# Eight of block 1's first products of layer 1 set among block 0's, their h kept where layer 2's weights will lie

## The chip, the cores and the metric

The kernel runs on one core of a Trainium2 chip. The metric is the device time of one launch in microseconds (us). Engines work from queues of their own, in the order in which the program lists each engine's instructions, and wait for each other by semaphores: PE does matrix products into PSUM, ACT and DVE do the work on single elements, SP issues the transfers (DMA). The profile's names are used throughout: PEld is PE's load of the fixed operand, which runs beside a product before it.

## The reference

`x` has the shape (2, 4096, 192), in single precision; the weights of the two layers come in double precision.

```python
w = softmax(weight, axis=-1)                   # (8 heads, 7 taps)
x_pad = pad(x, 6 zeros ahead of each sequence)
conv[b, s, h, g] = sum_k w[h, k] * x_pad[b, s + k, h, g]   # causal, 24 channels of a head
x = conv.reshape(8192, 192)

g = x @ w_gate                                 # layer 1: 192 -> 1536
x = (g * sigmoid(g) * (x @ w_val)) @ w_out     # 1536 -> 192

h = x @ w_in                                   # layer 2: 192 -> 2048
out = where(h > 0, h, exp(min(h, 0)) - 1) @ w_out2         # 2048 -> 192
```

## The kernel before

**Tiling.** Tokens lie along the free axis, channels on the partitions. The 8192 tokens are 16 blocks of `TB` = 512. Layer 1 of a block has 12 units of 128 of the 1536 middle channels, layer 2 has 16 units, taken two by two. Every operand of a product is split in a high and a low part of the number format `fp32r` (hi, lo), and a product is hi·hi + lo·hi + hi·lo.

**Couples.** A product of PE uses 64 of the 128 rows of the array. Two of them, one for the lower 64 rows and one for the upper, run side by side and write to two banks; this pair of matmuls is called a couple. A layer-1 unit has 9 couples of *first products* (`nine`, L362: gate columns into bank `pg`, value columns into `pv`), and 5 couples of *second products* (`ten`, L405) which add the unit's part to the block's four sums `c`. Between them stand silu (ACT L672), the gate (DVE L676), h hi (ACT L646) and h lo (DVE L650). A pair of layer-2 units has 9 couples into two banks `ph`, then per unit tanh (L706) and exp (L710) on ACT, `less` (L714) and `bound` (L718) on DVE, h hi and lo, and 2 x 5 couples of second products.

**Room.** PSUM has four banks `a` for first products (two units or pairs in flight) and four for `c`. Parts of h have a ring of 5 tiles each, `t` one of 4. A block's operand, hi and lo, has three homes.

**Weights.** They come as 34 pieces: 12 of W1 (first products of layer 1, one per unit), 6 of O1 (second products, one per two units), 8 of W2 and 8 of O2 for layer 2. SP brings a piece's words (L262) into a ring of 4; ACT and DVE make the parts from them: scale (ACT L266), three (ACT L289), join (DVE L293), sign (DVE L274), then hi (ACT L298) and lo (DVE L301). The pieces come in the order O1 0, W1 0, W1 1, W1 2, W1 3, O1 1, W1 4, ... and those of layer 2 last, W2 and O2 in turn.

**Order.** Layer and block follow in stages (1,0), (1,1), (1,2), (2,0), (2,1), (1,3), (2,2), (1,4), (2,3), ... up to (1,15), (2,14), (2,15). PE's order is fixed as the code writes it; for ACT, DVE and SP a planner places each instruction when by its costs its operands are there, the one with the longest tail first. Second products go through the list `due`: after each unit's first products all but the newest entry of `due` are written; at a stage's last unit before a layer-2 stage (`hold`) none are, so that they fill the first pairs of that stage. The convolution of block 1, taps (L576) and the operand's parts (L449, L453, L473, L477), stands in block 0's stage, that of block 2 in block 1's.

In the text, A b.j is a unit's first products in block b of layer 1, o b.j its second products, and E b.k a pair's first products of layer 2. PE's order at the start is A0.0, A0.1, A0.2, o0.0, A0.3, o0.1, ... A0.11, A1.0 and so on to A2.11, and then E0.0, o2.9, o2.10, E0.1, o2.11, E0.2.

Of the kernel before, what the change touches and what calls it, by code (L numbers as in the profile page):

```python
# [18 lines left out]
TB = 512  # L19
SLOTS = (0, 2, 1)  # L20
LEAD = 3
AIDED = 1
PATIENCE = 0.05
EPS = 2.0**-16
SPARED = range(0, 34)


def raw(ap):
    return ap.bitcast(F32)
# [103 lines left out]
def tile_conv_swiglu_elu(ctx: ExitStack, tc: tile.TileContext, x, weight, words, out, FF1, FF2):  # L133
# [10 lines left out]
    NU = {1: FF1 // P, 2: FF2 // P}  # L144
    assert D == P + HALF and TB % 2 == 0
    C = 2 * D
# [21 lines left out]
    plan = Plan()  # L168

    def act(emit, needs=(), new=(), uses=(), pitch=0.52, ready=0.68):  # L170
        return plan.add("act", pitch, ready, emit, needs, new, uses)

    def dve(emit, needs=(), new=(), uses=(), pitch=0.61, ready=0.74):
        return plan.add("dve", pitch, ready, emit, needs, new, uses)
# [72 lines left out]
    ready = {}  # L247

    def piece(k, moves, halves, serves):
# [34 lines left out]
        def three():  # L284
# [3 lines left out]
            w = box["st"].bitcast(U32)[:, :, 0]  # L288
            nc.scalar.activation(out=w, in_=w, func=AF.Copy, scale=2.0**-29 * (1 - EPS), bias=7.5 * EPS - 0.5)  # L289

# [122 lines left out]
    W1, W2 = Into("in1", NU[1]), Into("in2", NU[2] // 2)  # L413
    O = {1: OutOf("out1", NU[1]), 2: OutOf("out2", NU[2])}
# [145 lines left out]
    def conv(b, g):  # L560

        n = blocks[b][2]
        m, c0 = ((n, 0), (n // 2, HALO + TB))[g]
        src, src_b, came = xs[b]
        acc_b = plan.buffer("cv", 2)
        box = {}

        def tap(k):
            s = src["t"][:, c0 + k : c0 + k + m]
            w = taps[:, g, k : k + 1]  # L570
            if k == HALO:
                box["acc"] = cv_p.tile([P, TB], F32, tag="cv", name=f"cv{b}_{g}")
                nc.scalar.mul(box["acc"][:, :m], s, w)
                return
            acc = box["acc"][:, :m]
            nc.vector.scalar_tensor_tensor(out=acc, in0=s, scalar=w, in1=acc, op0=ALU.mult, op1=ALU.add)  # L576

        less = 0.0 if g == 0 else 0.27
        t = act(lambda: tap(HALO), [made, *came[g]], new=[acc_b], uses=[src_b], pitch=0.62 - less, ready=0.78 - less)
        for k in range(HALO):  # L580
            t = dve(lambda k=k: tap(k), [t], uses=[src_b, acc_b], pitch=0.67 - less, ready=0.8 - less)
        if g == 0:
            if b not in X:
                X[b] = Operand(f"x{b}", home["x", b])
            X[b].write(0, lambda: box["acc"][:, :n], [t], [acc_b], n)
        else:
            X[b].spread(lambda: box["acc"], t, acc_b, n)
# [29 lines left out]
    live = {}  # L617
    parts = {}
    split_of = {}
    sums = {}  # L620
    turns = {"last": None}

    def func(t):

        if turns["last"]:
            t.behind.append(turns["last"])
        turns["last"] = t
        return t

    def load_table(f):  # L630
        func(act(lambda: table(f), pitch=1.3, ready=1.3))

    def split(u):

        layer, b, j = u
        n = blocks[b][2]
        t_b, done = live[u][1:]
        bufs = [plan.buffer(f"h{q}", 5) for q in ("hi", "lo")]
        parts[u] = [None, None]

        def make(q):
            parts[u][q] = h_p.tile([P, TB], F32R, tag=f"h{'hi lo'.split()[q]}", name=f"h{q}_{layer}_{b}_{j}")

        def hi():
            make(0)
            nc.scalar.copy(parts[u][0][:, :n], live[u][0]["t"][:, :n])  # L646

        def lo():
            make(1)
            nc.vector.tensor_tensor(  # L650
                out=parts[u][1][:, :n], in0=live[u][0]["t"][:, :n], in1=raw(parts[u][0][:, :n]), op=ALU.subtract
            )

        h = act(hi, [done], new=[bufs[0]], uses=[t_b])
        l = dve(lo, [done, h], new=[bufs[1]], uses=[bufs[0], t_b])
        split_of[u] = bufs, (h, l)

    def swiglu(b, j):

        n = blocks[b][2]  # L660
        ps_b = [plan.buffer("a", 4) for _ in range(2)]
        t_b = plan.buffer("t", 4)
        box = {}

        def banks():
            if "p" not in box:
                box["p"] = [ps_a.tile([P, TB], F32, tag="a", name=f"p{q}{b}_{j}") for q in "gv"]
            return box["p"]

        def silu():  # L670
            box["t"] = t_p.tile([P, TB], F32, tag="t", name=f"t1_{b}_{j}")
            nc.scalar.activation(out=box["t"][:, :n], in_=box["p"][0][:, :n], func=AF.Silu)  # L672

        def gate():
            t = box["t"][:, :n]
            nc.vector.tensor_tensor(out=t, in0=t, in1=box["p"][1][:, :n], op=ALU.mult)  # L676

        last = W1.nine(ps_b, banks, j, X[b], n)[-1]
        s = func(act(silu, [last], new=[t_b], uses=ps_b[:1], pitch=0.49, ready=0.64))
        m = dve(gate, [last, s], uses=[ps_b[1], t_b])  # L680
        live[1, b, j] = box, t_b, m
        split((1, b, j))
# [46 lines left out]
    def products_out(u):  # L729
        layer, b, j = u  # L730
        n = blocks[b][2]
        if j == 0:
            second = [plan.buffer("c", 4) for _ in range(2)]
            acc_b[layer, b] = [plan.buffer("c", 4) for _ in range(2)] + second
        tasks = O[layer].ten((layer, b), acc_b[layer, b], j, u, n)
        if j == NU[layer] - 1:
            (middle if layer == 1 else finish)(b, *tasks)
# [88 lines left out]
    products(1)  # L826
    load_table(AF.Silu)

    due = []
    for i, (layer, b) in enumerate(stages):  # L830
        if i + 1 < len(stages) and stages[i + 1][0] == 1:
            if i:
                load_x(stages[i + 1][1])
            conv(stages[i + 1][1], 0)
            if i >= AIDED:
                conv(stages[i + 1][1], 1)
        if i and stages[i - 1][0] != layer:
            load_table(AF.Silu if layer == 1 else AF.Exp)
        for j in range(0, NU[layer], layer):
            swiglu(b, j) if layer == 1 else elus(b, j // 2)  # L840

            hold = layer == 1 and j == NU[1] - 1 and i + 1 < len(stages) and stages[i + 1][0] == 2
            while len(due) > 1 and not hold:
                for u in due.pop(0):
                    products_out(u)
            due.append([(layer, b, j + a) for a in range(layer)])
    for us in due:
        for u in us:
            products_out(u)

    plan.run({"pe": 1.0, "act": 0.8, "dve": 1.0, "pool": 2.3, "sp": 0.8}, PATIENCE)


# [43 lines left out]
```

## Time and profile before

| | us |
|---|---|
| median of 3 runs | 1224.89 (1224.43 to 1225.32) |
| the profiled execution | 1225.62 |
| its span | 1223.9 |
| PE busy | 1207.8 (99%) |
| DVE busy | 981.4 (80%) |
| ACT busy | 833.7 (68%) |
| chain that ended last: PE's part | 92% |

```profile
PE   7999999999999999999999999999999999999998
PEclk9999999999999999999999999999999999999999
DVE  7999899788595986959779596895968869495697
```

Each digit is the busy share of a fortieth of the span (30.6 us) in tenths. PE stands still only in the first slice, which holds the start of the program and the first weights; from there on it is busy at full clock. A time without PE's work can be saved only where PE waits.

### The profile page before, as it was taken

What the parts mean: (1) busy time and instruction counts of PE and PEld (TensorE: products, weight loads), DVE (VectorE), ACT (ScalarE), POOL (GpSimd) and SP (SyncE); (2) the same over time, 40 slices, a digit from 0 to 9 for tenths busy, and PEclk for the clock granted to TensorE, in tenths of its full rate; (3) what the DMA queues carried; (4) which work ended last, traced back from release to release, by engine and by line L of the source; (5) the groups of instructions that cost most, each with busy time, mean ns of one, the idle gap of its engine ahead of it and who ended that gap; (6) DMA issues with size and microseconds to landing.
All of it is one profiled execution on the core that took longest, in us unless ns stands there. A gap on an engine that the chain in (4) does not pass through costs nothing.

```text
span 1223.9 us, 25338 instructions
## 1 busy us (share of the span) xinstructions
PE 1207.8 (99%) x10272; PEld 968.8 (79%) x10272; DVE 981.4 (80%) x1631; ACT 833.7 (68%) x1556; POOL 2.1 (0%) x15
## 2 busy tenths in 40 slices
PE   7999999999999999999999999999999999999998
PEld 5778888888888888788887888878878788888876
DVE  7999899788595986959779596895968869495697
ACT  6979687486583856748576484765848667485676
POOL 0000000000000000000000000000000000000000
PEclk9999999999999999999999999999999999999999
DMA  6644020202020020201102011020200102000000
GB/s 174 192 128 125 15 44 14 66 18 53 1 44 27 18 53 8 49 15 25 47 10 48 14 36 36 18 53 1 44 14 18 40 1 47 12 18 14 18 11 18
DMA packets 34917, 48.65 MB, mean 40 GB/s; under 512 B 5872, under 2 KB 19696, under 8 KB 34800
## 3 DMA queue, kind: packets, MB, share of 16 engines
q1 hardware_dynamic: 34784, 47.04, 15.1%
q8 instruction: 80, 1.31, 0.5%
q14 instruction: 37, 0.30, 0.1%
q10 hardware_dynamic: 16, 0.00, 0.0%
HBM read 19.75 MB, written 6.29 MB: 21 GB/s over the span
## 4 chain that ended last, share of the span: by engine, by line
PE 92%; DVE 3%; ACT 2%; SPq 1%; DMA 1%; issue 1%; ACTq 0%; DVEq 0%
PE c L405 40%; PE pv L362 30%; PE ph L362 21%; DMA words<-in_words_dram 1%; SPq L262 1%; DVE t L714 1%; DVE t L718 1%; PE pg L362 0%; DVE w L293 0%; DVE h L650 0%; ACT w L266 0%; DVE t L676 0%; ACT words L289 0%; SPq L518 0%; DVE in1lo L301 0%
## 5 line engine op out<-in xcount | busy, mean ns | idle before, releaser
L405 PE MATMUL c<-h,out 64*128 64x512 f32 x4480 | 639.4, 392 | 0.5 <-DVE o L755 0.4
L405 PEld LDWEIGHTS c<-h,out 64*128 64x128 f32 x4480 | 472.9, 185 | 104.6 <-DVE o L755 4.1
L646 ACT CAST h<-t 128x512 fp32r<-128x512 f32 x448 | 278.7, 623 | 175.3 <-DVE t L676 126.8
L362 PE MATMUL pg<-x,in1hi 64*128 64x512 f32 x1152 | 391.0, 393 | 2.9 <-ACT in1hi L298 2.3
L362 PE MATMUL pv<-x,in1hi 64*128 64x512 f32 x1152 | 391.1, 393 | 0.8 <-DVE t L676 0.8
L650 DVE TENSOR_TENSOR h<-t,h 128x512 fp32r<-128x512 f32 x448 | 307.6, 687 | 93.9 <-ACT h L646 91.2
L362 PE MATMUL ph<-y,in2hi 64*128 64x512 f32 x1536 | 317.6, 391 | 0.0
L362 PEld LDWEIGHTS ph<-y,in2hi 64*128 64x128 f32 x1536 | 236.7, 185 | 35.5 <-DVE t L718 0.6
L362 PEld LDWEIGHTS pv<-x,in1hi 64*128 64x128 f32 x1152 | 213.2, 185 | 49.3 <-DVE t L676 1.2
L362 PE MATMUL ph<-y,in2lo 64*128 64x512 f32 x768 | 238.3, 391 | 0.0
L362 PE MATMUL pg<-x,in1lo 64*128 64x512 f32 x576 | 226.7, 394 | 2.0 <-DVE in1lo L301 2.0
L676 DVE TENSOR_TENSOR t<-t,pv 128x512 f32<-128x512 f32 x192 | 131.3, 684 | 119.2 <-ACT t L672 119.0
L362 PE MATMUL pv<-x,in1lo 64*128 64x512 f32 x576 | 226.7, 394 | 0.0
L362 PEld LDWEIGHTS pg<-x,in1hi 64*128 64x128 f32 x1152 | 213.3, 185 | 7.5 <-ACT in1hi L298 4.1
L672 ACT ACTIVATE t<-pg 128x512 f32<-128x512 f32 x192 | 114.4, 596 | 148.1 <-PE pg L362 145.9
L714 DVE SCALAR_TENSOR_TENSOR t<-t,th 128x512 f32<-128x512 f32 x256 | 175.2, 685 | 9.8 <-ACT t L710 9.1
L718 DVE SCALAR_TENSOR_TENSOR t<-ph,t 128x512 f32<-128x512 f32 x256 | 171.8, 686 | 3.0
L706 ACT ACTIVATE th<-ph 128x512 f32<-128x512 f32 x256 | 153.7, 600 | 24.1 <-PE ph L362 23.1
L362 PEld LDWEIGHTS ph<-y,in2lo 64*128 64x128 f32 x768 | 141.2, 185 | 16.5
L710 ACT ACTIVATE t<-ph 128x512 f32<-128x512 f32 x256 | 154.0, 601 | 0.0
L362 PEld LDWEIGHTS pv<-x,in1lo 64*128 64x128 f32 x576 | 106.7, 185 | 24.4
L362 PEld LDWEIGHTS pg<-x,in1lo 64*128 64x128 f32 x576 | 106.7, 185 | 5.4 <-DVE in1lo L301 4.2
(56 smaller groups left out, 528.2 us busy)
## 6 DMA issues: line engine op xcount, KB each, us to landing
x<-x SPq DMA_DIRECT2D x64, 128.0 KB, 3.2
y<-y SPq DMA_DIRECT2D x64, 128.0 KB, 2.3
words<-in_words_dram SPq DMA_DIRECT2D x14, 384.0 KB, 3.4
words<-in_words_dram SPq DMA_DIRECT2D x40, 128.0 KB, 2.8
x<-x SPq DMA_DIRECT2D x64, 64.0 KB, 2.0
out_dram<-o SPq DMA_DIRECT2D x16, 256.0 KB, 2.0
xs<-in_x_dram SPq DMA_DIRECT2D x14, 259.0 KB, 3.1
words<-in_words_dram SPq DMA_DIRECT2D x40, 64.0 KB, 2.5
```

Of the source, the lines that this page charges most:

```text
L262: nc.sync.dma_start(out=to[r, g], in_=w[r_in, g_in])
L362: nc.tensor.matmul(p[:, :n], w[r, k, s], m[r, s, :n], start=i == 0, stop=i == len(seq) - 1)
L405: nc.tensor.matmul(p[:, :n], lhs[r], m[r, :n], start=start, stop=stop)
L646: nc.scalar.copy(parts[u][0][:, :n], live[u][0]["t"][:, :n])
L650: nc.vector.tensor_tensor(out=parts[u][1][:, :n], in0=live[u][0]["t"][:, :n], in1=raw(parts[u][0][:, :n]), op=ALU.subtract)
L672: nc.scalar.activation(out=box["t"][:, :n], in_=box["p"][0][:, :n], func=AF.Silu)
L676: nc.vector.tensor_tensor(out=t, in0=t, in1=box["p"][1][:, :n], op=ALU.mult)
L706: nc.scalar.activation(out=own["th"][:, :n], in_=box["p"][a][:, :n], func=AF.Tanh, scale=0.5)
L710: nc.scalar.activation(out=own["t"][:, :n], in_=box["p"][a][:, :n], func=AF.Exp)
L714: nc.vector.scalar_tensor_tensor(out=t, in0=t, scalar=1.0, in1=th, op0=ALU.add, op1=ALU.mult)
L718: nc.vector.scalar_tensor_tensor(out=t, in0=box["p"][a][:, :n], scalar=0.0, in1=t, op0=ALU.max, op1=ALU.min)
```

## The change

`JOINED` is 4. In place of the loop's first two stages a function `both_first` writes them: after each first product of block 0 one entry of `due` (the second products of the unit before) is written, and from unit 4 on a first product of block 1 follows, so that eight of block 1's units (0 to 7) stand among block 0's. Their parts of h go into no ring but into `held` places in the storage of layer 2's weights: even units into the first four pieces' hi and lo of W2, odd ones into O2. `give_back` then makes the hi and lo instructions of those 12 pieces wait for the users of that h. After that the remaining four units of block 1 and everything else are written with `settle_due`, which writes at most two entries of `due` per unit of layer 1, and one per pair of layer 2, and stops after a block's last unit.

```diff
--- before.py
+++ after.py
@@ -21,6 +21,7 @@
 LEAD = 3
 AIDED = 1
 PATIENCE = 0.05
+JOINED = 4
 EPS = 2.0**-16
 SPARED = range(0, 34)
 
@@ -617,6 +618,7 @@
     live = {}
     parts = {}
     split_of = {}
+    held = {}
     sums = {}
     turns = {"last": None}
 
@@ -635,10 +637,15 @@
         layer, b, j = u
         n = blocks[b][2]
         t_b, done = live[u][1:]
-        bufs = [plan.buffer(f"h{q}", 5) for q in ("hi", "lo")]
+        kept = u in held
+        bufs = [{"users": []} if kept else plan.buffer(f"h{q}", 5) for q in ("hi", "lo")]
         parts[u] = [None, None]
 
         def make(q):
+            if kept:
+                flat, i = held[u][q]
+                parts[u][q] = flat[:, i * TB : (i + 1) * TB]
+                return
             parts[u][q] = h_p.tile([P, TB], F32R, tag=f"h{'hi lo'.split()[q]}", name=f"h{q}_{layer}_{b}_{j}")
 
         def hi():
@@ -826,8 +833,68 @@
     products(1)
     load_table(AF.Silu)
 
+    spare = [
+        (name, q, w.rearrange(form), size)
+        for name, q, w, form, size in (
+            ("in2", 0, W2.hi, "p n s c -> p (n s c)", C),
+            ("in2", 1, W2.lo, "p n s c -> p (n s c)", C),
+            ("out2", None, O[2].w, "p n c -> p (n c)", 2 * C),
+        )
+    ]
+    for j in range(NU[1] - JOINED):
+        half = j // 2
+        held[1, 1, j] = (
+            ((spare[0][2], half), (spare[1][2], half)) if j % 2 == 0 else ((spare[2][2], j - 1), (spare[2][2], j))
+        )
+
+    def give_back():
+
+        for u, places in held.items():
+            for (flat, i), buf in zip(places, split_of[u][0]):
+                name, q, _, size = next(p for p in spare if p[2] is flat)
+                for k in range(i * TB // size, ((i + 1) * TB - 1) // size + 1):
+                    his, los = ready[name, k * (1 if name == "in2" else 2)]
+                    for t in (his if q == 0 else los if q == 1 else his + los):
+                        t.needs += buf["users"]
+
     due = []
+
+    def settle_due(most=2):
+
+        while len(due) > 1 and most:
+            us = due.pop(0)
+            for u in us:
+                products_out(u)
+            most = most - 1 if us[-1][2] < NU[us[-1][0]] - 1 else 0
+
+    def both_first():
+
+        conv(1, 0)
+        done = 0
+        waiting = []
+        for j in range(NU[1]):
+            swiglu(0, j)
+            if due:
+                for u in due.pop(0):
+                    products_out(u)
+            due.append([(1, 0, j)])
+            if j >= JOINED:
+                swiglu(1, done)
+                waiting.append([(1, 1, done)])
+                done += 1
+        load_x(2)
+        conv(2, 0)
+        conv(2, 1)
+        due.extend(waiting)
+        for j in range(done, NU[1]):
+            swiglu(1, j)
+            due.append([(1, 1, j)])
+            settle_due()
+
+    both_first()
     for i, (layer, b) in enumerate(stages):
+        if i < 2:
+            continue
         if i + 1 < len(stages) and stages[i + 1][0] == 1:
             if i:
                 load_x(stages[i + 1][1])
@@ -840,14 +907,14 @@
             swiglu(b, j) if layer == 1 else elus(b, j // 2)
 
             hold = layer == 1 and j == NU[1] - 1 and i + 1 < len(stages) and stages[i + 1][0] == 2
-            while len(due) > 1 and not hold:
-                for u in due.pop(0):
-                    products_out(u)
+            if not hold:
+                settle_due(2 if layer == 1 else 1)
             due.append([(layer, b, j + a) for a in range(layer)])
     for us in due:
         for u in us:
             products_out(u)
 
+    give_back()
     plan.run({"pe": 1.0, "act": 0.8, "dve": 1.0, "pool": 2.3, "sp": 0.8}, PATIENCE)
```

All lines below the first of the diff stand one lower in the new kernel, those behind `split` seven lower (L362 becomes L363, L405 L406, L676 L683, L650 L657).

By order PE's start now reads A0.0, A0.1, o0.0, A0.2, o0.1, A0.3, o0.2, A0.4, o0.3, A1.0, A0.5, o0.4, A1.1, ... A0.11, o0.10, A1.7, A1.8, o0.11, A1.9, o1.0, o1.1, A1.10, o1.2, o1.3, ... up to A2.11, then E0.0, o2.9, E0.1, o2.10, E0.2, o2.11, E0.3.

PE after the second products of block 0's unit 3 before (names: `pg0_6` is the bank of block 0's unit 6, `x00` block 0's operand hi):

```order
L405 MATMUL c1_0_1_344<-h1_1_0_3_482,out1_118 128x512
L405 MATMUL c1_0_2_345<-h1_1_0_3_482,out1_118 128x512
L405 MATMUL c1_0_3_346<-h1_1_0_3_482,out1_118 128x512
L362 MATMUL pg0_6_537<-x00_193,in1hi_114 128x512
L362 MATMUL pv0_6_538<-x00_193,in1hi_114 128x512
L362 MATMUL pg0_6_537<-x00_193,in1lo_115 128x512
L362 MATMUL pv0_6_538<-x00_193,in1lo_115 128x512
```

and now (`x10` is block 1's operand hi):

```order
L406 MATMUL c1_0_1_309<-h1_1_0_3_475,out1_118 128x512
L406 MATMUL c1_0_2_310<-h1_1_0_3_475,out1_118 128x512
L406 MATMUL c1_0_3_311<-h1_1_0_3_475,out1_118 128x512
L363 MATMUL pg1_0_501<-x10_235,in1hi_114 128x512
L363 MATMUL pv1_0_502<-x10_235,in1hi_114 128x512
L363 MATMUL pg1_0_501<-x10_235,in1lo_115 128x512
L363 MATMUL pv1_0_502<-x10_235,in1lo_115 128x512
```

Where unit 6 of block 0, with its own piece of W1, followed, unit 0 of block 1 follows, whose piece was made for block 0's unit 0.

DVE at the start before, from in1lo of the second piece on (`w3_250` is the piece of W1 for unit 2, which is made into `in1lo`, `cv1_0` block 1's convolution, `t1_0_0` unit 0 of block 0 between its two products):

```order
L301 TENSOR_TENSOR in1lo_115<-w1_216,in1hi_114 128x384
L293 SCALAR_TENSOR_TENSOR w3_250<-w3_250,words3_186 128x384
L274 SCALAR_TENSOR_TENSOR w3_250<-words3_186,w3_250 128x384
L576 SCALAR_TENSOR_TENSOR cv1_0_176<-xs1_143,taps_106,cv1_0_176 128x512
L301 TENSOR_TENSOR in1lo_115<-w3_250,in1hi_114 128x384
L576 SCALAR_TENSOR_TENSOR cv1_0_176<-xs1_143,taps_106,cv1_0_176 128x512 x2
L676 TENSOR_TENSOR t1_0_0_284<-t1_0_0_284,pv0_0_228 128x512
L576 SCALAR_TENSOR_TENSOR cv1_0_176<-xs1_143,taps_106,cv1_0_176 128x512
L650 TENSOR_TENSOR h1_1_0_0_317<-t1_0_0_284,h0_1_0_0_303 128x512
```

and now:

```order
L302 TENSOR_TENSOR in1lo_115<-w1_216,in1hi_114 128x384
L577 SCALAR_TENSOR_TENSOR cv1_0_176<-xs1_143,taps_106,cv1_0_176 128x512 x4
L683 TENSOR_TENSOR t1_0_0_276<-t1_0_0_276,pv0_0_228 128x512
L294 SCALAR_TENSOR_TENSOR w3_284<-w3_284,words3_186 128x384
L657 TENSOR_TENSOR h1_1_0_0_306<-t1_0_0_276,h0_1_0_0_298 128x512
L275 SCALAR_TENSOR_TENSOR w3_284<-words3_186,w3_284 128x384
L683 TENSOR_TENSOR t1_0_1_314<-t1_0_1_314,pv0_1_270 128x512
L454 TENSOR_TENSOR x11_243<-cv1_0_176,x10_235 128x512
L302 TENSOR_TENSOR in1lo_115<-w3_284,in1hi_114 128x384
L294 SCALAR_TENSOR_TENSOR w4_332<-w4_332,words4_254 128x384
L275 SCALAR_TENSOR_TENSOR w4_332<-words4_254,w4_332 128x384
L657 TENSOR_TENSOR h1_1_0_1_358<-t1_0_1_314,h0_1_0_1_339 128x512
```

The four last taps of block 1's convolution stand ahead of that piece's join, and the gates of units 0 and 1 ahead of most of its work; the pieces behind it follow closer.

PE at a switch from layer 1 to layer 2 (block 7's last second products, `y60` is block 6's operand of layer 2) before:

```order
L405 MATMUL c1_7_2_7208<-h1_1_7_9_7513,out1_118 128x512
L405 MATMUL c1_7_3_7209<-h1_1_7_9_7513,out1_118 128x512
L405 MATMUL c1_7_2_7208<-h0_1_7_10_7542,out1_118 128x512
L405 MATMUL c1_7_3_7209<-h0_1_7_10_7542,out1_118 128x512
L405 MATMUL c1_7_2_7208<-h0_1_7_10_7542,out1_118 128x512
L405 MATMUL c1_7_3_7209<-h0_1_7_10_7542,out1_118 128x512
L405 MATMUL c1_7_0_7206<-h0_1_7_10_7542,out1_118 128x512
```

and now:

```order
L406 MATMUL c1_7_2_7194<-h1_1_7_9_7497,out1_118 128x512
L406 MATMUL c1_7_3_7195<-h1_1_7_9_7497,out1_118 128x512
L363 MATMUL ph6_2_7584<-y60_6782,in2hi_116 128x512
L363 MATMUL ph6_3_7585<-y60_6782,in2hi_116 128x512
L363 MATMUL ph6_2_7584<-y60_6782,in2lo_117 128x512
L363 MATMUL ph6_3_7585<-y60_6782,in2lo_117 128x512
L363 MATMUL ph6_2_7584<-y61_6999,in2hi_116 128x512
```

The second products of unit 10 have left the place ahead of the second pair's first products (`ph6_2`, `ph6_3`), which now follow those of unit 9 directly. This stands so at each of the 14 switches.

## Rows read from the trace of the kernel before

**Rows 1.** Windows; columns: PE, PEld, DVE, ACT, POOL busy, PEclk, DMA share, GB/s

```profile
50.00:100.00 50.00, 48.48 (x407) 37.96 (x405) 47.55 (x92) 39.38 (x83) 0.00 (x0) 1.00 0.56 151
70.00:130.00 60.00, 59.84 (x516) 48.18 (x514) 59.32 (x119) 47.81 (x101) 0.00 (x0) 1.00 0.43 117
```

**Rows 2.** Waits of PE up to 110 us: total, times, longest

```profile
PE pg L362 <- ACT in1hi L298: 2.3, 3, 1.5
PE pg L362 <- DVE in1lo L301: 2.0, 5, 0.5
...
PE pv L362 <- DVE t L676: 0.8, 1, 0.8
```

**Rows 3.** Waits of PE from 110 us to the end

```profile
PE c L405 <- DVE o L755: 0.4, 1, 0.4
```

**Rows 4.** Timeline of PE, two switches: start, duration, instruction

```profile
621.20 0.62 PE L362 MATMUL ph<-y,in2hi 64*128 64x512 f32 x2
...
695.84 0.39 PE L362 MATMUL pv<-x,in1hi 64*128 64x512 f32 x1
695.84 0.62 PE L362 MATMUL ph<-y,in2hi 64*128 64x512 f32 x2
```

**Rows 5.** Timeline of PE, from its first unit to layer 2's first pair

```profile
15.41 0.49 PE L362 MATMUL pg<-x,in1hi 64*128 64x512 f32 x1 [1.53 <-ACT in1hi L298]
...
38.26 0.39 PE L362 MATMUL pg<-x,in1hi 64*128 64x512 f32 x1
...
138.63 0.63 PE L362 MATMUL ph<-y,in2hi 64*128 64x512 f32 x2
```

**Rows 6.** Timeline of DVE in the first 42 us

```profile
6.49 4.68 DVE L576 SCALAR_TENSOR_TENSOR cv<-xs,taps,cv 128x512 f32<-128x512 f32 x6
...
18.11 0.56 DVE L301 TENSOR_TENSOR in1lo<-w,in1hi 128x384 fp32r<-128x384 f32 x1
...
40.09 0.68 DVE L650 TENSOR_TENSOR h<-t,h 128x512 fp32r<-128x512 f32 x1
40.70 0.68 DVE L676 TENSOR_TENSOR t<-t,pv 128x512 f32<-128x512 f32 x1
41.29 0.55 DVE L301 TENSOR_TENSOR in1lo<-w,in1hi 128x384 fp32r<-128x384 f32 x1
41.76 0.55 DVE L293 SCALAR_TENSOR_TENSOR w<-w,words 128x384 int32<-128x384 int32 x1
```

**Rows 7.** Timeline of ACT and of SP's queue, the words of the weights

```profile
28.27 0.55 ACT L289 ACTIVATE words<-words 128x384 uint32<-128x384 uint32 x1 [1.40 <-DMA words<-in_words_dram]
17.70 9.71 SPq L262 DMA_DIRECT2D words<-in_words_dram  x14
```

**Rows 8.** Timeline of PE and of PEld at the third unit's start

```profile
21.94 0.39 PE L362 MATMUL pg<-x,in1hi 64*128 64x512 f32 x1
23.10 0.49 PE L362 MATMUL pv<-x,in1hi 64*128 64x512 f32 x1 [0.77 <-DVE t L676]
23.10 0.18 PEld L362 LDWEIGHTS pv<-x,in1hi 64*128 64x128 f32 x1 [1.20 <-DVE t L676]
```

**Rows 9.** Windows of 1 us, columns as in rows 1

```profile
16.00:17.00 1.00, 0.60 (x3) 0.51 (x5) 1.00 (x2) 0.96 (x3) 0.00 (x0) 0.64 0.41 86
19.00:20.00 1.00, 1.00 (x8) 0.90 (x8) 0.96 (x3) 0.23 (x1) 0.00 (x0) 0.66 0.56 155
```

**Rows 10.** Timeline of the switch that begins at 695.84

```profile
696.75 1.28 ACT L190 ACT_TABLE_LOAD   x1
697.94 2.73 PE L405 MATMUL c<-h,out 64*128 64x512 f32 x20
701.82 0.69 DVE L718 SCALAR_TENSOR_TENSOR t<-ph,t 128x512 f32<-128x512 f32 x1
703.54 0.62 PE L362 MATMUL ph<-y,in2hi 64*128 64x512 f32 x2
```

**Rows 11.** The page's groups; out<-in, count, busy, mean ns, idle before

```profile
L646 ACT CAST h<-t 128x512 fp32r<-128x512 f32 x448 | 278.7, 623 | 175.3 <-DVE t L676 126.8
```

## The prediction

> **What bounds the kernel now.** I read first the windows of the middle: from 50 to 100 us PE is busy 48.48 of 50 at granted clock 1.00, from 70 to 130 it is 59.84 of 60 [rows 1]. Then PE's waits: after 110 us one single wait of 0.4 us is left [rows 3], and before that waits for weights in the making, 2.3 for in1hi and 2.0 for in1lo, and 0.8 for a gate [rows 2]. So PE bounds it, and only its start has something to give.
>
> How much follows from PE's pace. From the first pair of one layer-2 stage at 621.20 to that of the next at 695.84 PE does one round: 12 units of layer 1 with 9 + 5 couples and 8 pairs of layer 2 with 9 + 10, 320 couples in 74.64 us, 0.23325 each [rows 4]. From the first couple at 15.41 to layer 2's first at 138.63 [rows 5] PE has 36 first products of 9 couples and 33 second products of 5, together 489. At the pace these are 114.1 us; the stretch took 123.2. So 9 us are lost here, and the question is which of them the new order gets back. Behind 138.63 nothing is to be had: the couples are the same 5120 in all, PE does not wait, and the chain at the end holds the same instructions.
>
> Where in the stretch: at 38.26 block 0's unit 6 begins [rows 5], with 6 first and 4 second products done, 54 + 20 = 74 couples. The other 415 take 96.8 at the pace and would end at 135.06; the switch comes at 138.63. So 3.57 us are lost after 38.26, mostly for pieces of W1: PE needs a new one every 14 couples (9 + 5), sooner than ACT and DVE make them along with their other work. The remaining 5.5 are lost before it.
>
> **The change, part by part.**
>
> *Block 1's units among block 0's.* From A0.5 on, a new piece of W1 is needed only every 23 couples (9 + 5 + 9), 5.36 us, in place of every 14. What DVE has to do in such a period: two units with a gate and an h lo, each 0.61 to the next instruction (40.09 to 40.70, 40.70 to 41.29 [rows 6]), that is 2.4; a piece of W1 with join, sign and in1lo, the last 0.47 (41.29 to 41.76), together 1.41; half a piece of O1, 0.75 by the same steps. Sum 4.56, under 5.36. So the 3.57 go, if the start before them isn't later.
>
> *The start, worked out row by row in DVE's new order.* The order puts the second products of unit 0 directly behind A0.1, a lag of one unit in place of two, and on DVE four taps ahead of the piece of W1 for unit 2. In1lo of the piece before ends at 18.67 [rows 6]. Four dependent taps at 0.77 (six took 4.68 [rows 6]) with the instructions between end by 21.5; the gate of unit 0, join, h lo end at 23.6, so o0.0 goes on until 24.7 with PE idle from 21.94 (the end of A0.1's issue, as before [rows 8]) to about 22.95 and 0.6 more inside o0.0. In1lo of that piece ends at 25.75, A0.2 at 27.8, o0.1 at 28.9, A0.3 at 31.0. Then comes a wait that the change adds: DVE's join of the piece for unit 4 stands ahead of the gate of unit 2, and its words land at 28.27, when ACT's wait of 1.40 for them ends [rows 7]. ACT takes 0.55 and 0.53 for it, so join ends at 29.3, gate 2 at 29.8, h hi at 31.7 (0.62 on ACT [rows 11] behind other casts), h lo at 32.6; behind that join stand gate and h of units 2 and 3, and PE waits for them in o0.2, which ends at 33.2. A0.4 ends at 35.3, o0.3 at 36.46. There 5 first and 4 second products are done, 65 couples. The rest, 424, take 98.9 at the pace: the switch at 135.36 if PE waits no more. Before, 138.63: 3.27 less. (By 74 couples the new order is 0.3 behind the old one, and then loses none of the 3.57.)
>
> *What may eat it.* DVE has little in hand. From in1lo at 18.67 to the gate of A2.10 its new order has 209 steps, which by the steps above (81 products of 0.6, 16 taps of 0.74, the conversions 0.47 each or less for their smaller shapes) come to 112.2 us: 130.9, and the switch needs it by 135.4. Of these 4.5 us about 3.05 are spent by 46 us on waits for words and for PE, so 1.4 stay. Already before, DVE is busy 59.32 of 60 from 70 to 130 [rows 1]. In a queue in order some of that turns up on PE: at best nothing, at worst so much that the whole 3.27 is gone; I take 0.3, since the sum still closes before the switch.
>
> *The clock.* After PE stood still ahead of 15.41, the granted clock was 0.64 from 16 to 17 and 0.66 from 19 to 20 [rows 9], the lower level of 1.2 GHz beside the full one of 2.4, and by the middle it is 1.00 [rows 1]. The new order stands 1.0, 0.6, 0.2 and 0.75 us between 21.9 and 32. If the clock falls again, some 3 us of PE run at half speed, of which waits swallow part; 0.6 stay, with one chance in three, 0.2 on the average (inside the 0.3 above, with what waits hide).
>
> By the Trainium skill (TensorE: Matmul & The Clock Gate, section HAM oscillation — how this bites in real kernels) idle gaps put PE's clock down in the midst of a kernel. The trace agrees for the start, with 0.64 behind a wait of 1.53 us; whether the smaller gaps do it no row shows. By the rule the sum would be 0.6 worse, and still a gain.
>
> *The third pair of each layer-2 stage.* `settle_due(1)` writes one second product per pair, so between E.0 and E.2 (a stage's first and third pair) stand o9 and o10 and no longer o11. E.2 begins 9 + 5 + 9 + 5 = 28 couples or 6.53 us after E.0 by the pace, and it writes to E.0's banks, which the second `bound` of E.0 frees. In the switch at 695.84 that ends at 702.51, 6.67 after it [rows 10]; the table load of 1.28 on ACT sets it. Before, E.2 began at 703.54, 7.70 after: 1.0 in hand. Now 0.14 is missing. But a couple's upper half runs one couple behind the lower (pv of the last unit starts together with ph of the pair, at 695.84 [rows 4]), and the bank that comes late is the upper half's, which so needs it 0.23 later than 6.53. By that nothing is missing; should the halves be drawn together by the wait, up to 0.1 is. I take 0.02 a switch, near the rows' answer of nothing, 0.3 for 14. If the whole couple waits, it is 0.14 + 0.05 until the release is seen + 0.10 for a restart, 0.285 each, 4.0 in all.
>
> The 0.10 is from a start after a wait: the product at 23.10 took 0.49, the one before it 0.39, and its weight load had waited to 23.10 as well [rows 8]. The Trainium skill (TensorE: Matmul & The Clock Gate, section Architectural detail: the array is 16× 32×32, not 1× 128×128) says that PE pulls weight loads ahead of products in flight. By that alone a restart would cost nothing and the whole-couple case 2.6 in place of 4.0; here the load waited with its product, and the measured 0.10 decides.
>
> *Rooms.* The 12 pieces of layer 2 wait for h that PE has read by about 97 us; by the old places they are due from 135 on. Cost nothing; cover some 40 us.
>
> **Sum.** -3.27 + 0.3 + 0.3 = -2.7 on the profiled execution's 1225.62 (span 1223.9): 1222.9. It stands 0.73 above the median of the runs, 1224.89; so the median is forecast at 1222.1.
>
> **Rivals.**
>
> *A: DVE, not PE, sets the stretch from 36 to 135 us, or the clock falls again.* For it: 59.32 of 60 [rows 1] and the 1.4 in hand; against it, that much of that work is made ahead for layer 2 and can stand later. DVE then gives the switch at 136 to 137: gain 1.0 to 2.2, 1222.7 to 1223.9.
>
> *B: E.2 waits at every switch.* For it: 6.53 against 6.67. Against it: the halves. Whole couples waiting cost 4.0: -3.27 + 0.3 + 4.0 = +1.0, which is 1225.9 as a median. It decides from 0.21 a switch on, (3.27 - 0.3) / 14. If the pairs behind it (E.3, E.5, E.7), which wait for banks in the same way, each slip by 0.1 more, it is 0.45 to 0.6 a switch, 6.3 to 8.4 in all: 1228 to 1230, slower.
>
> *C: the head gives nothing.* The shorter lag of o0.0 turns waits for weights into waits for h: PE stands 2.5 us in the first 33 already. If this goes on over unit 4 and beyond (every later h waits for words as unit 2's does), the 3.57 are taken by it: 1224 to 1225.
>
> *D: layer 2's weights come late*, because the rooms hold h: the first W2 pieces would have to slip by 40 us. Then above 1226; nothing in the rows speaks for it.
>
> **How the numbers follow.** My forecast has 0.47, A 0.27, B 0.13 (0.05 within, 0.08 slower), C 0.10, D 0.03. The likeliest gives 1222.1. About 0.2% (2.45 us) can be told from no change: faster means under 1222.4. Of the forecast's own spread (1220.9 to 1223.0) four fifths lie under it, 0.38; of A nothing to little, 0.04; and a further 0.08 stand for more of the 5.5 us before 38 got back than I reckon. Faster 0.50; slower the 0.08 of B and 0.03 of D and 0.01 of C, 0.12; within 0.38. The range from 1220.7 to 1225.7 holds A, C and my case but for its ends, and leaves out B's worse part, D and a head much better than reckoned.
>
> **What would show it.** In the changed profile: the first `ph` at about 135.4 (A: 136 to 137; C: 138); PE's waits between 40 and 110 under 0.5; a wait of E.2 for `bound` L725 of under 0.05 at a switch (B: 0.2 or more, 14 times); PEclk at 1.00 after 21 (else a fall between 26 and 30); o0.2 waiting for h about 0.75. I am wrong if the switch comes at 135 and the end does not move: then B or something behind 135 that I haven't seen.

## The result and the profile after

The changed kernel is slower: 1235.28 us (median, 1233.33 to 1235.70) against 1224.77 (1224.43 to 1225.32), a ratio of 1.0081 with the interval 1.0069 to 1.0092. I had forecast 1222.1, faster, with a range up to 1225.7. Its profiled span is 1233.9.

The first thing to read is when layer 2 begins. PE's timeline in the changed kernel (start, duration, instruction):

```profile
139.49 0.62 PE L363 MATMUL ph<-y,in2hi 64*128 64x512 f32 x2
```

It was 138.63 before [rows 5] and I expected 135.36. So the start gained nothing, and 9 us more are lost behind it, where I had seen nothing to lose. PE's waits in the changed kernel, over the whole span (engine, line, releaser: total, times, longest), which answer to [rows 2, 3]:

```profile
PE c L406 <- DVE o L762: 1.9, 4, 0.5
PE c L406 <- ACT h L653: 1.8, 2, 0.9
PE pg L363 <- ACT t L679: 1.3, 1, 1.3
PE pg L363 <- ACT in1hi L299: 1.1, 1, 1.1
PE pg L363 <- DVE in1lo L302: 1.0, 2, 0.5
...
PE c L406 <- DVE p L762: 0.5, 1, 0.5
PE ph L363 <- DVE t L725: 0.4, 2, 0.2
```

The waits for weights fell from 4.3 to 2.1 [rows 2], which is what the change does. In their place stand waits for h and for a silu. Yet behind 139 us this view adds up to 2.8, of 9. PE has products in flight while the next one waits, so a wait of some tenths often isn't listed. What finds them is the pace: the start of a stage's first product, less 15.41, less the couples done until then at 0.23325 each (the pace of rows 4). The difference of two such values is what PE lost in between. By parts of the span, in us, with the experiments below it (a small negative number is a pace just under 0.23325: -1.4 over the 2280 couples of 15 stages is 0.2326 each). Each row is one profiled execution; that of e1 took 1226.65, 2.1 more than its median, the others stand within 1.2 of theirs:

| kernel | first ph at | lost before it | in layer-2 stages | at returns to layer 1, and in its stages | last stage | all |
|---|---|---|---|---|---|---|
| before | 138.63 | 9.2 | -1.4 | 0.3 | 0.6 | 8.7 |
| after | 139.49 | 10.0 | 4.8 | 4.0 | -0.2 | 18.7 |
| e1_old_lag | 139.13 | 9.7 | -0.7 | 0.0 | 0.7 | 9.7 |
| e2_rule_alone | 140.22 | 10.8 | 4.6 | 4.0 | -0.2 | 19.2 |
| e3_catch_up | 138.21 | 8.8 | 4.0 | 1.6 | 0.0 | 14.3 |
| e4_x_late | 136.84 | 7.4 | -1.5 | -0.2 | 0.6 | 6.2 |
| e5_lag_two | 136.29 | 6.8 | -1.5 | 0.3 | 0.6 | 6.2 |
| e6_rule_light | 138.78 | 9.3 | -1.0 | 1.3 | -0.2 | 9.4 |
| e7_rule_evict | 140.05 | 10.6 | 4.9 | 1.4 | -0.2 | 16.7 |
| e8_x_late_alone | 137.49 | 8.0 | -1.2 | -0.3 | 0.6 | 7.2 |

So there are three places, and each has its rows.

**The start.** ACT's timeline of the changed kernel:

```profile
57.01 0.55 ACT L267 ACTIVATE w<-words 128x384 f32<-128x384 f32 x1
60.56 0.54 ACT L290 ACTIVATE words<-words 128x384 uint32<-128x384 uint32 x1 [3.01 <-DMA words<-in_words_dram]
61.01 0.60 ACT L653 CAST out<-t 128x512 fp32r<-128x512 f32 x1
61.52 0.59 ACT L679 ACTIVATE t<-pg 128x512 f32<-128x512 f32 x1
```

and PE's:

```profile
62.16 0.50 PE L363 MATMUL pg<-x,in1hi 64*128 64x512 f32 x1 [1.28 <-ACT t L679]
```

The words' way to it, in the timeline of SP's queue and in the chain of waits of this stretch:

```profile
46.64 1.54 SPq L519 DMA_DIRECT2D xs<-in_x_dram  x3
48.29 2.58 SPq L263 DMA_DIRECT2D words<-in_words_dram  x4
50.97 0.53 SPq L519 DMA_DIRECT2D xs<-in_x_dram  x1
51.61 2.59 SPq L263 DMA_DIRECT2D words<-in_words_dram  x4
54.24 1.24 SPq L519 DMA_DIRECT2D xs<-in_x_dram  x2
55.59 10.80 SPq L263 DMA_DIRECT2D words<-in_words_dram  x8
```

```profile
55.59 4.95 DMA words<-in_words_dram
```

ACT stands for 3 us before the words of piece 17, the last of O1. Behind it in ACT's queue are an h of block 1 and the silu of A0.8, which frees a bank `pg`; PE's A0.9 waits for that bank. The Trainium skill (TensorE: Matmul & The Clock Gate, section Architectural detail: the array is 16× 32×32, not 1× 128×128) says that ACT's queue is strictly first in, first out; these rows agree, since a silu whose product was ready stood behind a wait that has nothing to do with it. The words are late, in part, because SP has taken the x of blocks 2 and 3, six loads, ahead of them: they are issued at 55.59, where before, with one of the six ahead, it was 50.92. Block 1's operand is made earlier in the new order, which frees room for block 3's x; that the planner moved the loads for this reason is not shown.

ACT's queue does the same at 34.41: it waits 2.04 for the words of piece 8, with h hi of unit 3 behind it, and PE loses 1.0 at o0.3. There it is not x that stands ahead of the words, but four copies within block 1's operand:

```profile
26.96 3.47 SPq L491 DMA_DIRECT2D x<-x  x4
30.54 0.52 SPq L263 DMA_DIRECT2D words<-in_words_dram  x1
```

Before, these words were issued at 26.88, ahead of such copies. What is lost after 65 us, 1.3, is lost mostly at the first second products of blocks 1 and 2 (85 and 113 us), which wait for the sums `c` of the block before.

**The layer-2 stages.** PE, ACT and DVE of the changed kernel at the pair E.5 of block 6:

```profile
565.79 0.65 ACT L713 ACTIVATE th<-ph 128x512 f32<-128x512 f32 x1
...
568.90 0.60 ACT L717 ACTIVATE t<-ph 128x512 f32<-128x512 f32 x1
...
569.88 0.60 ACT L717 ACTIVATE t<-ph 128x512 f32<-128x512 f32 x1
570.35 0.63 ACT L450 CAST y<-y 128x512 fp32r<-128x512 f32 x1
570.86 0.62 ACT L713 ACTIVATE th<-ph 128x512 f32<-128x512 f32 x1
...
571.59 0.69 DVE L725 SCALAR_TENSOR_TENSOR t<-ph,t 128x512 f32<-128x512 f32 x1
...
571.96 0.86 PE L363 MATMUL ph<-y,in2hi 64*128 64x512 f32 x2
572.33 0.49 PE L363 MATMUL ph<-y,in2lo 64*128 64x512 f32 x1
```

The second couple should start at 571.96 + 0.23 = 572.19. The `bound` that frees its bank ends at 572.28, it starts at 572.33, and takes 0.49 for 0.39. That is 0.14 + 0.10 = 0.24, and 12 of the 15 stages lose 0.24 to 0.29 there. In that of block 1 it is the sums `c` that cost 0.8, at the stage's first second products (187.89, behind the add `p`). In those of blocks 13 and 14 it is the pair E.3, whose bank E.1's `bound` frees; it loses 0.46 and 0.48:

```profile
1088.92 0.49 PE L363 MATMUL ph<-y,in2hi 64*128 64x512 f32 x1 [0.19 <-DVE t L725]
```

E.2, the pair that I had priced, loses 0.06 to 0.10 in 14 of the 15 stages, 1.2 in all. In the kernel before, the `bound` that E.5 of block 6 needs ended at 566.97, 0.87 ahead of the couple at 567.84:

```profile
565.69 1.28 DVE L718 SCALAR_TENSOR_TENSOR t<-ph,t 128x512 f32<-128x512 f32 x2
567.84 0.61 PE L362 MATMUL ph<-y,in2lo 64*128 64x512 f32 x2
```

Windows from E.0 to E.5, before and after (columns as in [rows 1]):

```profile
546.60:567.60 21.00, 21.00 (x183) 16.92 (x182) 17.73 (x29) 19.30 (x37) 0.00 (x0) 1.00 0.07 14
```

```profile
553.20:571.90 18.70, 18.70 (x162) 14.85 (x162) 15.62 (x25) 17.57 (x34) 0.00 (x0) 1.00 0.00 1
```

By order E.5 follows E.0 after 80 couples now and after 90 before, 18.7 us in place of 21.0. ACT is busy 17.57 of these 18.70, DVE 15.62; behind the table load ACT has pauses of 0.7 in all. In the rows above, E.3's exp stands 3.1 behind its tanh (565.79, 568.90): between them ACT makes two h and two parts of block 7's operand, work that is due as well.

**The returns to layer 1.** DVE and PE of the changed kernel where layer 2's sums of block 3 make room for block 5's:

```profile
369.98 0.68 DVE L683 TENSOR_TENSOR t<-t,pv 128x512 f32<-128x512 f32 x1
370.58 1.00 DVE L577 SCALAR_TENSOR_TENSOR cv<-xs,taps,cv 128x256 f32<-128x256 f32 x2
371.50 0.68 DVE L762 TENSOR_TENSOR p<-p,c 128x512 f32<-128x512 f32 x1
372.10 0.69 DVE L657 TENSOR_TENSOR h<-t,h 128x512 fp32r<-128x512 f32 x1
372.70 0.68 DVE L762 TENSOR_TENSOR o<-o,c 128x512 f32<-128x512 f32 x1
...
372.12 0.86 PE L406 MATMUL c<-h,out 64*128 64x512 f32 x5
373.43 0.96 PE L406 MATMUL c<-h,out 64*128 64x512 f32 x5 [0.45 <-DVE o L762]
```

PE's o1.5.0 starts at 372.12 and its second bank pair waits for the add `o`, which starts 0.58 later. Before, the same add started with the second products, at 368.12:

```profile
366.92 0.68 DVE L755 TENSOR_TENSOR p<-p,c 128x512 f32<-128x512 f32 x1
367.52 0.68 DVE L650 TENSOR_TENSOR h<-t,h 128x512 fp32r<-128x512 f32 x1
368.12 0.68 DVE L755 TENSOR_TENSOR o<-o,c 128x512 f32<-128x512 f32 x1
...
368.12 1.47 PE L405 MATMUL c<-h,out 64*128 64x512 f32 x9
```

The three instructions p, h, o stand in the same order in both kernels; it is the whole row that comes 0.58 later against PE. The loss is 0.7 to 0.8 at blocks 4 to 7 and 0.3 to 0.4 at block 3 and blocks 8 to 13; it was about 0.1.

The clock is in order: in the start the granted clock falls once, between 17 and 21 us (before: between 16 and 20), and is 1.00 from 21 on, with PE waiting 0.92, 0.22 and 0.49 between 22 and 26. Windows of the changed kernel, columns as in [rows 1]:

```profile
18.00:19.00 1.00, 1.00 (x8) 0.85 (x6) 0.97 (x3) 0.00 (x0) 0.00 (x0) 0.50 0.57 127
...
23.00:24.00 1.00, 0.65 (x4) 0.34 (x6) 0.89 (x2) 1.00 (x4) 0.00 (x0) 1.00 0.65 208
```

Not every execution has the fall there: the profiles of e2, e4 and e5 below have 1.00 from 16 to 21. In that of e3, whose order up to here is the same, PE waits 1.73 ahead of o0.0, and the clock falls behind that, between 24 and 28:

```profile
25.00:26.00 1.00, 1.00 (x8) 0.32 (x4) 1.00 (x3) 1.00 (x3) 0.00 (x0) 0.50 0.23 47
```

The Trainium skill (TensorE: Matmul & The Clock Gate, section HAM oscillation — how this bites in real kernels) tells of waits of PE that put its clock down in the midst of a kernel. The trace of e3 agrees, with 0.50 behind 1.73; in that of the changed kernel the three shorter waits took nothing.

### The profile page after: what moved, and what is told of

It reads as the page before. It is cut to its first block, busy times and chain, and to the rows that moved or that the text cites. A ratio compares the mean times of both kernels' runs of the same rounds, so it can differ in the third digit from the quotient of the medians.

```text
span 1233.9 us, 25410 instructions
## 1 busy us (share of the span) xinstructions
PE 1214.3 (98%) x10272; PEld 968.6 (78%) x10272; DVE 984.8 (80%) x1631; ACT 837.1 (68%) x1556; POOL 2.1 (0%) x15
## 4 chain that ended last, share of the span: by engine, by line
PE 71%; DVE 19%; ACT 4%; issue 3%; DMA 2%; SPq 1%; DVEq 0%; ACTq 0%
PE c L406 30%; PE pv L363 22%; PE ph L363 20%; DVE h L657 5%; DVE cv L577 4%; DVE t L721 2%; DVE t L725 2%; DMA words<-in_words_dram 2%; DVE t L683 2%; DVE x L478 1%; DVE p L762 1%; DVE x L454 1%; DVE o L762 1%; ACT words L290 1%; SPq L263 0%
## 5 line engine op out<-in xcount | busy, mean ns | idle before, releaser
L406 PE MATMUL c<-h,out 64*128 64x512 f32 x4400 | 628.0, 392 | 5.2 <-DVE o L762 1.9
L406 PEld LDWEIGHTS c<-h,out 64*128 64x128 f32 x4400 | 463.9, 185 | 109.8 <-DVE o L762 7.5
L653 ACT CAST h<-t 128x512 fp32r<-128x512 f32 x440 | 274.5, 626 | 177.5 <-DVE t L683 126.6
L363 PE MATMUL pg<-x,in1hi 64*128 64x512 f32 x1152 | 390.2, 393 | 2.4 <-ACT t L679 1.3
L363 PE MATMUL pv<-x,in1hi 64*128 64x512 f32 x1152 | 390.3, 393 | 0.3 <-DVE t L683 0.3
L657 DVE TENSOR_TENSOR h<-t,h 128x512 fp32r<-128x512 f32 x440 | 293.0, 685 | 87.6 <-ACT h L653 86.8
L363 PE MATMUL ph<-y,in2hi 64*128 64x512 f32 x1536 | 322.6, 393 | 0.5 <-DVE t L725 0.4
L363 PEld LDWEIGHTS ph<-y,in2hi 64*128 64x128 f32 x1536 | 234.3, 185 | 44.8 <-DVE t L725 12.0
L363 PEld LDWEIGHTS pv<-x,in1hi 64*128 64x128 f32 x1152 | 213.3, 185 | 47.3 <-DVE t L683 1.3
L363 PE MATMUL ph<-y,in2lo 64*128 64x512 f32 x768 | 241.1, 395 | 0.0
L683 DVE TENSOR_TENSOR t<-t,pv 128x512 f32<-128x512 f32 x192 | 131.3, 684 | 126.3 <-ACT t L679 126.1
L363 PE MATMUL pg<-x,in1lo 64*128 64x512 f32 x576 | 226.1, 393 | 1.0 <-DVE in1lo L302 1.0
L363 PE MATMUL pv<-x,in1lo 64*128 64x512 f32 x576 | 225.9, 392 | 0.0
L363 PEld LDWEIGHTS pg<-x,in1hi 64*128 64x128 f32 x1152 | 213.3, 185 | 7.3 <-ACT in1hi L299 1.9
L363 PEld LDWEIGHTS ph<-y,in2lo 64*128 64x128 f32 x768 | 138.7, 185 | 15.1
L363 PEld LDWEIGHTS pv<-x,in1lo 64*128 64x128 f32 x576 | 106.5, 185 | 23.5
L577 DVE SCALAR_TENSOR_TENSOR cv<-xs,taps,cv 128x512 f32<-128x512 f32 (+1 forms) x180 | 108.0, 620 | 1.8
```

The lines of the kernel that those rows point to most:

```text
L363: nc.tensor.matmul(p[:, :n], w[r, k, s], m[r, s, :n], start=i == 0, stop=i == len(seq) - 1)
L406: nc.tensor.matmul(p[:, :n], lhs[r], m[r, :n], start=start, stop=stop)
L657: nc.vector.tensor_tensor(out=parts[u][1][:, :n], in0=live[u][0]["t"][:, :n], in1=raw(parts[u][0][:, :n]), op=ALU.subtract)
```

## The experiments

The median of before is 1225.22 in the comparisons of e1 to e4 and 1225.03 in those of e5 to e8. Each ratio is against it.

**e1_old_lag.** Which half of the change costs?

```diff
-                settle_due(2 if layer == 1 else 1)
+                settle_due(9)
```

> The change with the old rule for second products behind the first two stages (all but the newest entry at each step); the joined units stay. By my theory the 10 us are lost in three places, and only the first belongs to the joined units: up to layer 2's first pair PE lost 10.0 us against its pace where it lost 9.2 before (+0.85), in the layer-2 stages +6.2 (banks of the pairs E.2 and E.5, which come too soon), at the switches back to layer 1 +3.7 (sums c evicted late). The last two go with the rule: then 1225 to 1226 here, first ph at about 139.4. Rival: the joined units (other rooms, other homes of the operands, an earlier plan) disturb every later stage and the rule costs little: 1232 to 1235.

1224.55 us, ratio 0.9997 (0.9988 to 1.0005). The losses behind the first ph are gone (the table's fourth and fifth column), those before it stay in its profile, with the same stop of PE for piece 17's words. The joined units disturb nothing behind them.

**e2_rule_alone.** In the kernel before, the loop's `while` is replaced by the new rule:

```diff
-            while len(due) > 1 and not hold:
-                for u in due.pop(0):
-                    products_out(u)
+            if not hold:
+                settle_due(2 if layer == 1 else 1)
```

> The kernel before with the new rule for second products alone (one entry per pair of layer 2, two per unit of layer 1, a stop after a block's last unit); no joined units, no rooms. My theory: the stages behind 139 us lose what the changed kernel loses there, 9 to 10 us: 1233 to 1235, with waits of ph for the bound (L725 in the changed kernel) and of c for the sums' add at every round. Rival (joined units disturb the later stages): 1225 to 1226.

1235.49, ratio 1.0082 (1.0068 to 1.0095): the same slowdown without a joined unit. The start is here 1.6 later than before though PE's order in it is hardly changed. So the planner's order of ACT and DVE, or one execution against the next, moves the start by about that much, and differences of the first column under 1.5 us say little.

**e3_catch_up.**

```diff
-                settle_due(2 if layer == 1 else 1)
+                settle_due(2 if layer == 1 or j >= 12 else 1)
```

> The change, but from the seventh pair of a layer-2 stage on two entries of second products are written per pair, so that at the switch back to layer 1 the lag is the old one. It parts the two later losses. If the late eviction of the sums c comes from the lag at that switch, the 3.7 us of it go and the 5 to 6 of the banks of E.2 and E.5 stay: about 1231.5. Rival: the planner's order there is an echo of the earlier part of the stage, and both stay: 1234 to 1235; or the bunch at the seventh pair makes a new wait there and nothing is won.

1231.26, ratio 1.0053 (1.0040 to 1.0065). The returns fall from 4.0 to 1.6: those of 0.7 to 0.8 are 0.1 to 0.2 now, those of 0.3 at blocks 8 to 13 are mostly still there (0.2 to 0.4). The losses at E.2, E.3 and E.5 stay; the 0.8 at block 1's sums went too. So the larger part of the late eviction comes from the lag at the return. What the rest comes from is not shown. The start's order for ACT and DVE is the changed kernel's up to 107 us, and yet layer 2 begins 1.3 earlier (138.21, 139.49): that much lies between two executions.

**e4_x_late.** With the old rule as e1, and

```diff
     give_back()
+    for b in (2, 3):
+        for group in xs[b][2]:
+            for t in group:
+                t.behind.append(came[17][-1])
```

> As the kernel with the old rule, and the loads of blocks 2's and 3's x stand on SP behind the words of the last piece of O1 (piece 17). In the changed kernel ACT waited 3.0 us for those words with a silu and an h behind it, and PE waited 1.4 and 0.7 for these (58.6 to 65 us). My theory: SP took six loads of x ahead of those words, some 3.4 us of issue; without them the words come 3 us sooner, the wait goes and the first ph comes about 2 us earlier than in the kernel with the old rule: 1223 to 1224. Rival: the words wait for their ring, and ACT's wait only moves to the next piece: no change against the old rule, 1225 to 1226.

1223.82, ratio 0.9989 (0.9981 to 0.9998). ACT's timeline of this kernel, the same instruction as above at 60.56:

```profile
56.29 0.53 ACT L290 ACTIVATE words<-words 128x384 uint32<-128x384 uint32 x1
...
57.77 0.58 ACT L679 ACTIVATE t<-pg 128x512 f32<-128x512 f32 x1
```

and PE's first pair of layer 2:

```profile
136.84 0.62 PE L363 MATMUL ph<-y,in2hi 64*128 64x512 f32 x2
```

ACT takes the words 4.3 us sooner, the silu of A0.8 starts at 57.77 in place of 61.52, and layer 2 begins 2.3 earlier than in e1's profile; up to 59 us both have lost the same 6.6. So the start's largest loss goes with the loads of x. But the order on SP is only part of it. In e3's profile the six loads stand ahead of the words as well, which are issued at 54.99; they land at 58.22, 3.2 later in place of 4.95, ACT waits 1.08, and PE loses nothing there:

```profile
58.24 0.56 ACT L290 ACTIVATE words<-words 128x384 uint32<-128x384 uint32 x1 [1.08 <-DMA words<-in_words_dram]
```

Some 1.7 of the 3.0 are thus the longer way of this one load, which not every execution has. The medians of e1 and e4 are 0.7 apart, and their runs overlap.

**e5_lag_two.** As e4, and in `both_first`

```diff
-            if due:
+            if len(due) > 1:
                 for u in due.pop(0):
```

> As the kernel with the old rule and the late loads of x, and second products among the joined units lag by two entries, as before the change, in place of one. In that kernel PE still waits 2.1 us ahead of and in o0.0 and 1.1 at o0.3, where an h stands behind ACT's wait for words. My theory: the shorter lag of the new start is what turns waits for weights into waits for h, so with the old lag a further 1 us or more goes: first ph at 135.5 to 136, 1222.5 to 1223. Rival: the words themselves are what is late, and PE waits for in1hi or in1lo in their place: no change, 1223.8.

1223.17, ratio 0.9986 (0.9977 to 0.9995). The loss at o0.3 falls from 1.1 to 0.1 and the first ph comes at 136.29, 0.55 earlier; less than the 1 us expected, since other places take some back (0.9 at block 1's first second products, where 0.5 was). It has the lowest median, and is faster than the kernel before by 0.14%; from e4 it can't be told, since the two intervals overlap and 0.55 in the first column says little.

**e6_rule_light.** As e2, and in `elus`

```diff
+            if k < 3:
+                m = func(act(exp, [last], new=[t_b], uses=[ps_b[a]], pitch=0.49, ready=0.64))
+            else:
...
             m = dve(bound, [m], uses=[t_b, ps_b[a]])
```

> The kernel before with the new rule alone, and in the first three pairs of each layer-2 stage tanh (ACT) and less (DVE) are left out: their h is min(max(h, 0), exp h). That takes six instructions of 0.6 from ACT and six of 0.6 from DVE in the stretch where pairs follow every 14 couples. Theory: the wait of the pair E.5 comes from that backlog of ACT and DVE (ACT is busy 17.97 of the 19.10 us from E.0 to E.5 in the changed kernel), so the 5 us that the layer-2 stages lose beyond the old kernel go, and the eviction's 4 at the switch to layer 1 stays: 1230 to 1231. Rival: the table load and the fixed distance of the pairs set it whatever the work: 1234 to 1235.

1227.27, ratio 1.0016 (1.0007 to 1.0025). E.2, E.3 and E.5 lose nothing any more (0.0 in all stages, after 0.24), though the pairs follow as closely as in e2 and the table load is where it was. So it is the amount of work of ACT and DVE that makes E.5's bank late. It is not a shorter chain: that bank is E.3's, and E.3 keeps tanh and less, yet in block 6 its last `bound` ends 4.5 behind its last product (564.12, 559.63), where it was 6.7 in the changed kernel (572.27, 565.58). E.2 and E.3 wait for banks of E.0 and E.1, whose own chain got shorter, and for these the run doesn't part the two. More went than expected: the returns at blocks 4 to 7 fell to 0.1 as well. Part of the late eviction is thus the same backlog carried on, or the planner's order after it; this run can't part these.

**e7_rule_evict.** As e2, and in `gathered`

```diff
             done.append((s, buf, box))
+            late = split_of.get((1, key[1] + 2, 1))
+            if key[0] == 2 and key[1] and late:
+                late[1][0].behind.append(c)
+                late[1][1].behind.append(s)
```

> The kernel before with the new rule alone, and the h hi and h lo of a layer-1 stage's second unit stand behind the copies and adds that evict the sums c of the layer-2 stage before it. Theory: of the rule's cost some 4 us come from DVE doing that h lo (0.6) ahead of the add for which the banks c wait: 1231 to 1232, and PE's waits at o.0 of layer 1 fall to the 0.1 of before. Rival: the add waits for the last second products themselves or for ACT's copies in any order: 1235.

1232.52, ratio 1.0062 (1.0048 to 1.0076). DVE at the same place:

```profile
371.24 0.68 DVE L755 TENSOR_TENSOR p<-p,c 128x512 f32<-128x512 f32 x1
371.83 0.68 DVE L755 TENSOR_TENSOR o<-o,c 128x512 f32<-128x512 f32 x1
372.43 0.68 DVE L650 TENSOR_TENSOR h<-t,h 128x512 fp32r<-128x512 f32 x1
```

The add now starts 0.08 after PE's second products (371.75), and the loss at blocks 4 to 7 is 0.1 to 0.2 where it was 0.8. At blocks 8 to 13 the planner put a tap in h lo's place, and 0.3 to 0.4 stayed. Of 4.0 at the returns 2.6 went. Since h lo stood ahead of that add in the kernel before too, the run shows that taking 0.6 out of the way pays for the delay, and not that h lo's place is its cause.

**e8_x_late_alone.** The late loads of e4 in the kernel before.

> The kernel before with the loads of blocks 2's and 3's x behind the words of piece 17 on SP, and nothing else. It parts what the late loads give by themselves from what they give with the joined units. Theory: before, PE waits for in1hi and in1lo that ACT and DVE make too slowly, and not for words; so little changes, 1224.5 to 1225.5. Rival: the words were late there too, and the gain of the kernel with late loads needs no joined units: 1223 to 1224.

1224.74, ratio 0.9996 (0.9987 to 1.0005): no difference that can be measured, although its profiled start is 1.1 earlier. e5, measured beside it, is 1.57 below it, so the gain of e5 needs the joined units. For e4, 0.92 below it but measured in another round, this is likely and not shown.

## Why the prediction was wrong

*What bounds the kernel* held: PE, and waits for weights at its start. *"Behind 138.63 nothing is to be had"* was read as "nothing is to be lost", and there the prediction failed. I took the absence of waits [rows 3] for slack. PE had none to wait for because ACT and DVE were just in time: the `o` add of the sums started in the same moment as the products that wait for it, and E.2 had 1.0 us in hand only thanks to the third second product between. A rule that moves PE's order at 14 switches has to be priced at all that follows there, and I priced E.2 alone.

*The third pair, 0.3.* The mechanism and its two parts were right, the banks and the halves one couple apart. E.2 lost 0.08 on the average over 15 stages, the restart's 0.10 without a wait to be seen, for the 0.02 that I took: 1.2 in place of 0.3; the bounds of 0 to 0.1 held. E.5 was missing from the sum, with 0.24 to 0.29 in 12 stages, and so were E.3 in two (0.46, 0.48) and the sums in that of block 1 (0.8): together 4.9 us. With E.2 this is what the layer-2 stages lost more than before, 6.2, some 0.4 a stage. It stood only in rival B, as the pairs that "each slip", 0.45 to 0.6 a switch, with 8 in 100. E.5 needs no bank that is late by itself: the second products that stood between the pairs were also ACT's and DVE's time to catch up, 2.3 us of it up to E.5.

*The returns to layer 1* were in no term and no rival: 3.7 us. The larger lag was passed over, because neither the number of couples nor the end of the span changes by it. It changes every return: the second products of four units in place of two follow A.0, and at blocks 4 to 7 the eviction of the sums comes half a microsecond later against PE.

*The start, -3.27.* The reckoning by couples and by DVE's steps was as far as it went near the chip: 36.46 at the end of o0.3 was 37.24. That is in part luck: of the 0.75 that I expected as a wait in o0.2 there was 0.3, and the 1.05 at o0.3 was not in the reckoning. The step that failed is "if PE waits no more", from 36.46 on. I followed one wait for words, that of the piece for unit 4, and none behind it; and I didn't follow SP, whose order the change also moves: six loads of x come ahead of words by which ACT waits. With those moved (e4) and the old lag (e5) the first ph comes at 136.29, and 2.3 of the 3.27 are there. Of these e8 has 1.1 without a joined unit, though its median doesn't show it; between the medians of e8 and e5 stand 1.57. So the joined units do about half of what they were said to do, and the rest of the new order kept it from being seen.

*The rival DVE* (A) was wrong in its engine: DVE's 4.5 us in hand did not decide, ACT's queue did, at 34 and at 60 us.

*The clock and the rooms* cost nothing in the changed kernel, as reckoned. In e3's execution the clock falls between 24 and 28, near the place where I gave a fall one chance in three; by 41 us 6.85 is lost there against the changed kernel's 6.66, so it cost some 0.2 at most.

What stays open: how much of the late eviction at the returns is backlog and how much the planner's choice (e3, e6 and e7 each remove the larger part in their own way), why one load of words takes 4.95 us in one execution and 3.2 in another, and why e5 still loses 6.8 us before layer 2, 5 of them before 30 us, where the first weights arrive.

## What to carry to other kernels

A view of waits that is empty says that everything comes in time, not by how much: before an order is moved, look for the instruction that came last at each such place and how early it was. Count the couples between two users of the same bank, before and after; the other engines must do the same work in that time. And follow every queue that the change reorders, down to the transfers, since an engine that takes its work in order passes a late transfer on to whatever stands behind it.

## What the runs showed of the hardware

A couple that just misses its bank costs more than the wait: PE's next couple takes 0.48 or 0.49 for 0.39, and 0.09 to 0.10 are lost even where no wait can be read (E.2 at 559.75: second couple at its due time, third 0.09 late). One load of words of 384 KB took 4.95 us from issue to landing in the chain of the changed kernel and 3.2 in e3, at the same place in the same order, with loads of x ahead of it; the median of such loads in the kernel before is 3.4. The granted clock's fall at the start comes and goes from one execution to the next: 0.50 for some microseconds in the profiles of both kernels, none in e2, e4 and e5. It cost the joined order nothing: at 24.2 us the changed kernel, with the fall, has lost 4.11 against the pace and e4, without it, 4.10, since PE then waits for h.
